# Splitting one product between VectorE and GpSimd, issuing two output matmuls earlier, and narrowing the last output piece

## The chip, the cores and the metric

The kernel runs on one core of a Trainium2 chip. The metric is the device time of one execution in microseconds; of several executions the median is given. The span in a profile is the time from the first to the last instruction of the profiled execution, about 1.8 us less than the device time of the same execution.

## The reference

An attention-like step feeds a two-layer block. Per batch (8) and head (8), with x of 512 x 64 and a state of 32 x 64:

```python
scores = scale * np.matmul(x, state.transpose(0, 1, 3, 2))
a = softmax(scores); xread = np.matmul(a, state)
scores2 = scale * np.matmul(state, x.transpose(0, 1, 3, 2))
a2 = softmax(scores2); sread = np.matmul(a2, x)
# rows of both, heads side by side: 4352 rows of 512
h = rows @ w_in                       # 512 -> 2048
g = h * (1.0 / (1.0 + np.exp(-h)))    # SILU
out = g @ w_out                       # 2048 -> 512
```

The softmax is shortened here; the rest is as in the reference, with the reshaping left out.

## The kernel before

The kernel folds the state into w_in ("W", one copy per batch), so that h is W times the normalised scores. G1 is the matmul of W with those scores, one step for each 128 of the 2048 hidden columns; G2 multiplies SILU(G1) by w_out and accumulates over the 16 steps. In batch 0 the whole chain has to start from nothing: load x, transpose, scores, exp, normalise, transpose, G1, SILU, G2. This ramp and the last output piece are what the change touches.

The normalisation; the argument `parts` says which engine multiplies which quarter:

```python
def norm(b, hg, parts=((nc.gpsimd, 0, 4),), nr=4):
    ...
    for c in range(0, 4, nr):
        nc.vector.tensor_reduce(rs[:, ds(c, nr)], e[:, ds(c, nr)], axis=AX, op=ADD)
    nc.vector.reciprocal(rc[:], rs[:])
    for eng, c, n in parts:
        eng.tensor_tensor(a[:, ds(c, n)], e[:, ds(c, n)],
                          rc[:, ds(c, n)].to_broadcast([128, n, 4, NS]), op=MULT)
```

The ramp of batch 0 (cut; `both` is VectorE for the first half and ScalarE for the second; `upto(k)` emits G1 steps until k of them have been emitted):

```python
norm(0, 0)                                  # first head half, on GpSimd
scores(0, 1, 2)
exps(0, 1)
norm(0, 1, ((nc.vector, 0, 4),), 2)         # second head half, on VectorE
...                                         # GpSimd issues weight and x loads
pss0 = w1_mms(0, [(128, 384)])
keep_busy(2, psH, "h1")                     # filler matmuls
for c in (0, 2):                            # transpose, copy out of PSUM
    ...; at_mms(ps_a, 0, 0, c, 2); copy(both[c // 2], aT[0][:, 0, ds(c, 2), :], ps_a[:])
for c in (0, 2):
    ...; at_mms(ps_a, 0, 1, c, 2); copy(nc.vector, aT[0][:, 1, ds(c, 2), :], ps_a[:])
w1_out(0, [(128, 128)], both, pss0)         # W for the second G1
upto(1)                                     # first G1: four steps of 256, two SILU halves
w1_out(0, [(128, 256)], (nc.vector, nc.vector), pss0, 128)
upto(2)                                     # second G1
for ft in range(12):
    upto(min(ft + LEAD0[ft], ready))
    ...
    for tt in range(3):
        G2(0, tt, ft)
```

The end:

```python
store(B, 0, nc.scalar)
last_cols(B, 1, 0, 256, nc.scalar, nc.sync)     # columns from, count, copy engine, queue
last_cols(B, 1, 256, 128, nc.vector, nc.scalar)
last_cols(B, 1, 384, 128, nc.vector, nc.sync)
```

The softmax here doesn't subtract the row's maximum and nothing guards it: scores larger than these inputs give would overflow.

## Time and profile before

| | before |
|---|---|
| device time, first three runs | 212.91 us (212.73 to 213.1) |
| span of the profile | 210.9 us |
| PE busy | 205.3 us (97%) |
| start of the third G1 (the end of the ramp) | 12.88 us |
| start of the last three pieces on PE | 203.95 us |
| issue of the last store | 208.00 us |

PE is busy nearly without a break, so the busy table alone says little. The profile's lines give start, duration, engine, source line, operation, output and inputs with their shapes, and a count. PE is TensorE's matmuls and PEld its weight loads, DVE is VectorE, ACT is ScalarE, POOL is GpSimd; SPq and ACTq are the queues that issue DMAs. Brackets say how long the engine stood idle just before and who released it.

### The profile page before, as it was taken

The numbers are of one execution on the slowest core, as the hardware profiler recorded it, in microseconds if no ns is written. First come the engines' busy times: TensorE is split into PE (matmuls) and PEld (weight loads), VectorE is DVE, ScalarE is ACT, GpSimd is POOL, SyncE is SP. The second block draws the span as 40 slices with busy tenths as digits, with TensorE's granted clock in tenths as the row PEclk, the third lists the DMA queues.
The fourth block names the chain that finished last, engine by engine and source line by source line (L and its number), as shares of the span: only waits on it lengthen the run. The fifth ranks groups of instructions, "written<-read, shape, count | busy, mean of one in ns | idle before, by whom it ended". The sixth has DMA issues, their size and how long they took to land.

```text
span 210.9 us, 3866 instructions
## 1 busy us (share of the span) xinstructions
PE 205.3 (97%) x1575; PEld 96.8 (46%) x1575; DVE 74.0 (35%) x146; ACT 139.2 (66%) x244; POOL 39.5 (19%) x62
## 2 busy tenths in 40 slices
PE   7899999999999999999999999999999999999993
PEld 2444354445444444444444544444444444466653
DVE  3851268567831336115211662043412306100011
ACT  3865677899577867697569855996775166644410
POOL 8681213704220402021201202000200000000000
PEclk9999999999999999999999999999999999999999
DMA  6999999995559475644925528115321111011112
GB/s 205 181 204 206 284 256 354 219 273 194 101 145 259 152 137 119 145 154 114 237 75 173 112 71 193 50 50 102 85 64 46 63 56 53 0 50 50 53 50 99
DMA packets 42929, 28.65 MB, mean 136 GB/s; under 512 B 28064, under 2 KB 37792, under 8 KB 42912
## 3 DMA queue, kind: packets, MB, share of 16 engines
q1 hardware_dynamic: 36720, 20.65, 37.7%
q0 software_dynamic: 5904, 7.64, 17.5%
q8 instruction: 12, 0.20, 0.4%
q10 hardware_dynamic: 288, 0.13, 0.2%
q14 instruction: 5, 0.04, 0.1%
HBM read 17.43 MB, written 8.91 MB: 125 GB/s over the span
## 4 chain that ended last, share of the span: by engine, by line
PE 95%; DMA 2%; DVE 1%; ACT 0%; issue 0%; DVEq 0%
PE o L566 51%; PE h L525 26%; PE ps_w L469 4%; PE h L546 3%; PE o_a L566 3%; DMA x_f<-in_x_dram 2%; PE o_part L588 2%; PE ps_sr L416 1%; PE ps_xt L253 1%; PE ps_sc L306 1%; PE ps_scT L332 1%; PE ps_busy L165 1%; PE ps_at L398 0%; PE h L507 0%; DVE W L159 0%; ACT xT L157 0%
## 5 line engine op out<-in xcount | busy, mean ns | idle before, releaser
L566 PE MATMUL o<-w_out_sb,g 128*128 128x512 bf16 x496 | 131.8, 379 | 0.0
L557 ACT ACTIVATE g<-h 128x512 bf16<-128x512 f32 (+1 forms) x143 | 81.2, 573 | 34.2 <-PE h L525 20.1
L566 PEld LDWEIGHTS <-g 128*128 128x128 bf16 x528 | 50.3, 98 | 59.0 <-issue 3.8
L525 PE MATMUL h<-aT,W 128*128 128x512 bf16 x254 | 74.5, 379 | 0.1
L159 DVE COPY o_sb<-o 128x512 f32<-128x512 f32 x15 | 10.4, 691 | 89.8 <-PE o L566 87.3
L525 PEld LDWEIGHTS <-W 128*128 128x128 bf16 x254 | 24.6, 98 | 30.5 <-issue 1.2
L159 DVE CAST W<-ps_w 128x512 bf16<-128x512 f32 (+2 forms) x36 | 22.2, 659 | 23.2 <-PE ps_w L469 23.2
L157 ACT ACTIVATE W<-ps_w 128x512 bf16<-128x512 f32 (+1 forms) x32 | 16.2, 562 | 11.1 <-PE ps_w L469 11.1
L159 POOL CAST x_nat<-x_f 128x512 bf16<-128x512 f32 x24 | 14.2, 631 | 35.9 <-DMA x_f<-in_x_dram 35.9
L157 ACT ACTIVATE o_sb<-o 128x512 f32<-128x512 f32 x16 | 9.5, 597 | 14.3 <-PE o L566 11.8
L362 POOL TENSOR_TENSOR an<-e,rcn 128x512 bf16<-128x512 bf16 x5 | 7.6, 1518 | 48.9 <-DVE rcn L360 39.3
L469 PE MATMUL ps_w<-w_in_sb,stT 64*32 64x512 bf16 (+2 forms) x264 | 10.1, 373 | 0.0
L566 PE MATMUL o_a<-w_out_sb,g 128*128 128x512 bf16 x32 | 10.0, 379 | 0.0
L546 PE MATMUL h<-xmT,w_in_sb 128*128 128x256 bf16 x64 | 9.6, 273 | 0.0
L546 PEld LDWEIGHTS <-w_in_sb 128*128 128x128 bf16 x64 | 6.3, 98 | 3.9
L165 PE MATMUL ps_busy<-busy 128*128 128x512 bf16 x16 | 5.8, 481 | 1.2 <-DVE warm L172 1.2
L359 DVE TENSOR_REDUCE rs<-e 128x32 f32<-128x1024 bf16 x5 | 6.1, 1211 | 2.1 <-DMA e<-eT 2.1
L346 ACT ACTIVATE eT<-ps_scT 128x512 bf16<-128x512 f32 x10 | 5.4, 594 | 1.6 <-PE ps_scT L332 1.6
L786 ACT ACT_TABLE_LOAD x5 | 6.4, 1283 | 0.1
L382 POOL TENSOR_TENSOR an<-exp_nat,rc 128x512 bf16<-128x512 bf16 x3 | 3.1, 1047 | 13.9 <-DMA x_f<-in_x_dram 8.7
L469 PEld LDWEIGHTS <-stT 64*32 64x32 bf16 x264 | 3.2, 90 | 5.2 <-issue 3.9
L768 ACT ACT_TABLE_LOAD x4 | 5.1, 1283 | 0.1
(76 smaller groups left out, 99.8 us busy)
## 6 DMA issues: line engine op xcount, KB each, us to landing
out_dram<-o_sb SPq DMA_DIRECT2D x33, 256.0 KB, 2.4
x_f<-in_x_dram SPq DMA_DIRECT2D x4, 1024.0 KB, 6.3
x_f<-in_x_dram POOLq DMA_DIRECT2D x2, 1024.0 KB, 12.6
w_in_sb<-in_moe_w_in_dram POOLq DMA_DIRECT2D x3, 512.0 KB, 10.2
x_f<-in_x_dram SPq DMA_DIRECT2D x2, 512.0 KB, 4.7
w_out_sb<-in_moe_w_out_dram POOLq DMA_DIRECT2D x4, 256.0 KB, 11.9
w_out_sb<-in_moe_w_out_dram POOLq DMA_DIRECT2D x2, 512.0 KB, 12.1
x_f<-in_x_dram POOLq DMA_DIRECT2D x2, 512.0 KB, 14.9
```

Source lines behind the costliest of these rows:

```text
L157: nc.scalar.activation(dst, src, func=COPY, bias=0.0)
L159: eng.tensor_copy(dst, src)
L165: nc.tensor.matmul(ps[:], busy[:, 0:128], busy[:], start=True, stop=True, skip_group_check=True)
L346: nc.scalar.activation(t[:, hg], scT_ps[hg][:], func=EXP, bias=0.0, scale=SCALE)
L359: nc.vector.tensor_reduce(rs[:], e2[b][:], axis=AX, op=ADD)
L362: eng.tensor_tensor(a[:, hg], e2[b][:, hg], rc[:, hg].to_broadcast([128, 4, 4, NS]), op=MULT)
L469: nc.tensor.matmul(pss[f, hg][ds(32 * s, 32), 0:n], stT[ds(r, 64), b, h // 2, s % 2, :], w_in_sb[ds(r, 64), h // 2, ds(f, n)], start=True, ...
L525: nc.tensor.matmul(h_ps[k][:], W1[b][:, hg, ds(128 * ft, 128)], aT[b][:, hg, :, :], start=(hg == 0), stop=(hg == 1), skip_group_check=True,)
L546: nc.tensor.matmul(ps[:, 0:256], w_in_sb[:, kt, ds(128 * ft, 128)], xmT[:, :, kt].rearrange("p t n b -> p t (n b)"), start=(kt == 0), stop ...
L557: nc.scalar.activation(g[:, 0:n], ps[:, 0:n], func=SILU, bias=0.0)
L566: nc.tensor.matmul(outs[tt][:], gt[b * NFT + ft][:, ds(128 * tt, 128)], w_out_sb[:, ft, :], start=(ft == 0), stop=(ft == NFT - 1), skip_gr ...
L786: nc.scalar.activation(warm[:], busy[:, 0:1], func=SILU, bias=0.0)
```

## The change

The intent: VectorE has a queue of work in the ramp, so GpSimd takes half of its second product; the first two G2 steps need only the first half of the first SILU, so they go ahead of the second G1; the last output piece is halved so that less is left to copy and store after the last matmul.

```diff
-    norm(0, 1, ((nc.vector, 0, 4),), 2)
+    norm(0, 1, ((nc.vector, 0, 2), (nc.gpsimd, 2, 2)), 2)
 ...
-    w1_out(0, [(128, 128)], both, pss0)
+    w1_out(0, [(128, 128)], (nc.vector, nc.vector), pss0)
     upto(1)
     w1_out(0, [(128, 256)], (nc.vector, nc.vector), pss0, 128)
+    G2(0, 0, 0)
+    G2(0, 1, 0)
     upto(2)
+    G2(0, 2, 0)
 ...
     for ft in range(12):
-        upto(min(ft + LEAD0[ft], ready))
+        if ft > 0:
+            upto(min(ft + LEAD0[ft], ready))
 ...
-        for tt in range(3):
+        for tt in range(3 if ft > 0 else 0):
             G2(0, tt, ft)
 ...
-    last_cols(B, 1, 256, 128, nc.vector, nc.scalar)
-    last_cols(B, 1, 384, 128, nc.vector, nc.sync)
+    last_cols(B, 1, 256, 192, nc.vector, nc.scalar)
+    last_cols(B, 1, 448, 64, nc.vector, nc.sync)
```

## The prediction

> **What bounds the kernel now.** I read the page first: busy shares, then the chain that ended last.
>
> ```profile
> PE 205.3 (97%) x1575; PEld 96.8 (46%) x1575; DVE 74.0 (35%) x146; ACT 139.2 (66%) x244; POOL 39.5 (19%) x62
> PE 95%; DMA 2%; DVE 1%; ACT 0%; issue 0%; DVEq 0%
> ```
>
> TensorE sets the time: 95% of the chain is PE. A change can therefore only move three things: how long PE waits in the ramp before its unbroken stream begins, the PE work itself, and what follows its last matmul. The change touches the first and the last. I took the ramp (10 to 15 us) and the end apart in narrow windows of the timeline. The ramp, engine by engine:
>
> ```profile
> 9.07 1.05 POOL L382 TENSOR_TENSOR an<-exp_nat,rc 128x512 bf16<-128x512 bf16 x1 [2.00 <-DVE rc L380]
> 9.97 0.70 DVE L382 TENSOR_TENSOR an<-exp_nat,rc 128x512 bf16<-128x512 bf16 x1
> 10.43 0.69 PE L398 MATMUL ps_at<-ident,an 128*128 128x128 bf16 x8
> 10.74 0.80 DVE L159 COPY aT<-ps_at 128x256 bf16<-128x256 bf16 x3
> 11.45 0.94 DVE L159 CAST W<-ps_w 128x128 bf16<-128x128 f32 x3
> 11.70 0.66 ACT L516 ACTIVATE g<-h 128x256 bf16<-128x256 f32 x2 [0.21 <-PE h L507]
> ```
>
> Columns are start, duration, engine, line, operation. GpSimd normalises the first head half until 10.12, VectorE the second until 10.67, PE transposes both, and VectorE copies the transposes out (ACT takes one copy and one W copy, not in these lines). The first half of SILU ends at 11.70+0.38 = 12.08. What PE does meanwhile:
>
> ```profile
> 11.09 0.79 PE L507 MATMUL h<-aT,W 128*128 128x256 bf16 x4
> 11.79 0.60 PE L525 MATMUL h<-aT,W 128*128 128x512 bf16 x2
> 12.23 0.59 PE L566 MATMUL o<-w_out_sb,g 128*128 128x512 bf16 x2
> 12.67 0.38 PE L566 MATMUL o_a<-w_out_sb,g 128*128 128x512 bf16 x1
> 12.88 1.03 PE L525 MATMUL h<-aT,W 128*128 128x512 bf16 x4
> ```
>
> The reader should see that the second G1 (11.79) lies exactly in the wait for that SILU. It ends its issue at 11.79+0.44 = 12.23, and the first G2 follows without a hole, though its input has been ready since 12.08. I take 12.88, the start of the third G1, as the mark of the ramp: from there PE hardly waits.
>
> **What the Trainium skill says.** (1) "GPSIMD Engine Reference", § 4.1 Engine selection, calls GpSimd about twice as slow as VectorE for elementwise work on two inputs, and its § 1 Specifications says that its SBUF interfaces are shared with VectorE, with contention where a VectorE instruction has two SBUF inputs. The trace agrees in direction: this product takes 1.05 us on GpSimd against 0.70 us on VectorE (1.5 times). Where both start together (59.17 us, VectorE first), VectorE keeps 0.69 and GpSimd takes 1.55; where GpSimd is already running (34.18), VectorE is stretched to 0.88. (2) "TensorE: Matmul & The Clock Gate", § Back-to-back issue gap, gives N/2.4 + 2.5 ns a step, but about 81 ns for pairs of weight load and matmul at N=128. In this trace the smaller figure holds: eight transposes of 128 columns take 0.45 us of the chain (56 ns each), two 512-column steps 0.43 (216 ns each), and eight 64-column steps, each with its own weight load, 30.78 to 31.01 = 29 ns each. (3) "DMA: Bandwidth & Descriptors", § Specifications, asks for at least 512 B for line rate; the new last piece has rows of 64 x 4 = 256 B. The last stores before have 512 B rows and land in 1.9 to 2.0 us, so no run yet shows what that costs.
>
> **Part 1: GpSimd takes half of the second product.** VectorE's half is 256 columns. Halving the streamed part (512 columns at 0.96 GHz-like pace is about 0.53 of the 0.70 us) gives 0.43, so it ends at 9.97+0.43 = 10.40 instead of 10.67. GpSimd starts its half at 10.1 after its own first product: half of 1.05 plus a little is 0.55 us, but VectorE holds the two-input read until 10.40. From the pair at 59.17 GpSimd does about 0.1 us of work in such an overlap, so it ends near 10.85 (10.65 with no contention).
> What it buys: PE reaches the transposes at 10.43 in any case, because before them stand a W product that waited for w_in until 9.70 (0.29 us of issue) and two fillers (0.43). The first transpose copy on VectorE needs the transposes' end, 10.70, so it stays at 10.74. The second copy started at 11.05, held by the product's end at 10.67; now it can follow the first at VectorE's 0.21 us spacing, 10.95. The third needs GpSimd's end plus 0.38 (the distance from product end to copy start above, 10.67 to 11.05), 11.23 against 11.26. So one copy comes 0.10 us earlier. The first h is complete at about 11.56 instead of 11.66 and its SILU runs 11.60 to 11.98. Gain on this step: 0.10 us.
> GpSimd's six weight and x issues start 0.55 to 0.8 us later. I expect that to be hidden: the weight loads issued at 5.1, 10.1 and 11.6 us land 9.8, 10.2 and 13.8 us after issue, which is a backlog growing in the queue, not an issue limit.
>
> **Part 2: both first W copies on VectorE.** ACT loses a copy of 0.27 us that ended at 11.49, before its SILU could start, so ACT gains nothing. VectorE's W copies for the second G1 now end at about 11.65 and 11.9. That G1 could start near its old time for one half and about 11.95 for the other.
>
> **Part 3: two G2 steps ahead of the second G1.** PE issues the last first-G1 step by about 11.70 and then waits for SILU: first G2 at 11.98+0.05 = about 12.04. Then two G2 (0.43) to 12.47, second G1 (0.43) to 12.90, third G2 (0.22) to 13.12. The third G1 starts at 13.12 instead of 12.88: **+0.24 us**. The same matmuls are done, but 0.43 us of them have been taken out of a hole that they filled, and only 0.19 us of that is won back (0.10 from part 1, about 0.09 from the hole's other edges). Everything behind the mark is PE stream. The w_in block for the next W product landed at 5.14+9.8 = 14.94 and PE used it at 14.99, so a gain in the ramp of over 0.05 us could not have passed this load anyway; a loss meets no slack and goes through to the end.
>
> **Part 4: 192 + 64 columns at the end instead of 128 + 128.**
>
> ```profile
> 206.79 0.29 DVE L159 COPY o_part<-o_part 128x128 f32<-128x128 f32 x1 [5.40 <-PE o_part L588]
> 207.11 0.64 ACTq L598 DMA_DIRECT2D out_dram<-o_part  x1
> 207.68 0.29 DVE L159 COPY o_part<-o_part 128x128 f32<-128x128 f32 x1 [0.60 <-PE o_part L588]
> 208.00 0.54 SPq L598 DMA_DIRECT2D out_dram<-o_part  x1
> ```
>
> PE before: 32 steps x 56 ns = 1.79 us. After: 16 x 82.5 (the skill's formula, an estimate) + 16 x 29 = 1.78 us, the same. The last matmul's latency falls from 219 to 193 ns (the 64-column rows show 193): 0.03. The last copy falls from 0.29 to an estimated 0.23 us (64 columns fewer at about 1 ns): 0.07. The last store carries 32 KB instead of 64; 128 KB landed in 2.1 and 64 KB in 1.9 to 2.0 us, so 0 to 0.1 less. Sum **-0.12 us**. The 192-column piece is copied by about 207.61 and issued at 207.64 on ACT's queue, landing near 209.7, just under the last piece's 209.8: close, but not the bound.
>
> **Sum.** +0.24 - 0.12 = +0.12 us: 212.91 becomes about 213.0.
>
> **The rivals.** A, *the change works as meant*: the split product is worth its full 0.27 us, the SILU comes as much earlier, and PE no longer stops for W copies. For it: VectorE is busy without a break from 10.74 to 12.4, so shortening its queue looks right. Against: PE's 10.43 and the load at 14.94 are not moved by it. It would make 212.6. B, *GpSimd is late*: contention as at 59.17 puts its half at 10.95 or later, the third copy and the second SILU half slip, and the delayed load issues make the W product at 20.85 wait (its w_in landed at 10.07+10.2 = 20.27, slack 0.58). For it: the measured 1.55 us. Against: the backlog. It would make 213.3 to 213.6. C, *narrow matmuls cost a full weight load*: if the last 16 steps took 56 ns instead of 29, PE ends 0.43 later and the sum is 213.5. Against it stand the 29 ns score steps. D, *256 B rows make the last store slow*: up to +0.2 in place of the gain, 213.2.
>
> **Range and chances.** The terms are tenths of a microsecond against run-to-run scatter of 0.37 us (212.73 to 213.1). A pulls down by 0.4, B and C up by about 0.5; with scatter I take 212.5 to 213.4. Two per cent is 4.3 us, which no rival comes near: same 0.98, faster 0.01, slower 0.01.
>
> **What would show it right or wrong.** Right: first G2 at about 12.04 with PE idle before it until SILU ends, third G1 near 13.12, the W product that stood at 14.99 near 15.23, last copy near 0.23 us, last 16 matmuls at 29 ns. Wrong: the third G1 at or before 12.88 (then A), a PE wait on w_in at 21 us (B), the last piece's matmuls spread over 0.9 us (C), a landing of the last store over 2.1 us (D).

## The result and the profile after

The changed kernel took 212.99 us (212.93 to 213.15, six runs) against 212.82 us (212.73 to 213.1, six runs) for the kernel before. The ratio is 1.0008, 95% interval 0.9995 to 1.0021: the same within 2%. Ratios here are the mean time of one kernel's runs over that of the other's of the same rounds, so they are not quite the ratio of the medians quoted. By time alone a loss is likely but not certain; where it would come from is read from the trace. First the page of the changed kernel, busy table and chain:

```profile
PE 205.9 (98%) x1575; PEld 96.9 (46%) x1575; DVE 74.2 (35%) x147; ACT 139.1 (66%) x243; POOL 40.4 (19%) x63
...
PE 95%; DVE 1%; POOL 1%; issue 0%; ACT 0%; POOLq 0%
```

PE still is 95% of the chain. In the chain's account, POOL (GpSimd) has come in where a DMA stood before. The ramp in the timeline, VectorE, GpSimd and ACT:

```profile
9.97 0.42 DVE L382 TENSOR_TENSOR an<-exp_nat,rc 128x256 bf16<-128x256 bf16 x1
10.08 0.79 POOL L382 TENSOR_TENSOR an<-exp_nat,rc 128x256 bf16<-128x256 bf16 x1
...
10.68 0.86 DVE L159 COPY aT<-ps_at 128x256 bf16<-128x256 bf16 x3 [0.28 <-PE ps_at L398]
11.46 1.14 DVE L159 CAST W<-ps_w 128x128 bf16<-128x128 f32 x4
11.56 0.73 ACT L516 ACTIVATE g<-h 128x256 bf16<-128x256 f32 x2 [0.23 <-PE h L507]
```

VectorE's product now ends at 10.39, but GpSimd's half ends at 10.87, later than VectorE's whole product did before (10.67). VectorE then waits 0.28 us for PE's transposes, and its three copies end where they did. The first SILU starts 0.14 us earlier. What PE makes of it:

```profile
11.05 0.81 PE L507 MATMUL h<-aT,W 128*128 128x256 bf16 x4
...
11.99 0.10 PEld L566 LDWEIGHTS <-g 128*128 128x128 bf16 x1 [0.52 <-ACT g L516]
11.99 0.60 PE L566 MATMUL o<-w_out_sb,g 128*128 128x512 bf16 x2
12.44 0.59 PE L525 MATMUL h<-aT,W 128*128 128x512 bf16 x2
12.87 0.38 PE L566 MATMUL o_a<-w_out_sb,g 128*128 128x512 bf16 x1
13.08 1.03 PE L525 MATMUL h<-aT,W 128*128 128x512 bf16 x4
```

The last step of the first G1 starts at 11.60 and PE can give way about 0.11 us later, the distance of two such steps; then nothing is left that may run until SILU has ended at 11.94. The first G2 starts at 11.99 after a hole of some 0.28 us, and the third G1 at 13.08 instead of 12.88. That 0.20 us is still there at the start of the last three pieces: 204.16 instead of 203.95. The end of the changed kernel:

```profile
207.42 0.36 DVE L159 COPY o_part<-o_part 128x192 f32<-128x192 f32 x1 [5.83 <-PE o_part L588]
207.81 0.64 ACTq L598 DMA_DIRECT2D out_dram<-o_part  x1
207.89 0.23 DVE L159 COPY o_part<-o_part 128x64 f32<-128x64 f32 x1
208.14 0.54 SPq L598 DMA_DIRECT2D out_dram<-o_part  x1
```

Counted from the start of the last three pieces, the last issue comes 3.99 us later; before it was 208.00 - 203.95 = 4.05. So 0.07 us is gained up to the issue (3.988 against 4.054 unrounded). But the span ends 7.00 us after that start, before 6.97: the gain is gone. (The page gives spans to 0.1 us; these two come from the packed traces, 211.156 - 204.156 and 210.921 - 203.949.) The DMA issues of the end (size, and time from issue to landing), first before, then changed:

```profile
out_dram<-o_part ACTq DMA_DIRECT2D x1, 64.0 KB, 2.0
out_dram<-o_part SPq DMA_DIRECT2D x1, 64.0 KB, 1.9
```

```profile
out_dram<-o_part ACTq DMA_DIRECT2D x1, 96.0 KB, 2.1
out_dram<-o_part SPq DMA_DIRECT2D x1, 32.0 KB, 2.0
```

The last store carries half as much and takes longer to land, 2.0 us after its issue instead of 1.9 (1.99 and 1.89 in the packed traces). The DMA activity between 207.5 and 211.5 us, one digit for 0.1 us, shows a candidate for why; before and changed:

```profile
DMA  5998200006950000069500000000000000000000
```

```profile
DMA  0059983000000000699982000000000000000000
```

Before, the last two stores are two separate bursts. In the changed kernel they have become one.

### The profile page after: what moved, and what is told of

It is laid out like the page before. It is cut to its first block, busy times and chain, and to the rows that moved or that the text cites. A ratio compares the mean times of both kernels' runs of the same rounds, so it can differ in the third digit from the quotient of the medians.

```text
span 211.2 us, 3868 instructions
## 1 busy us (share of the span) xinstructions
PE 205.9 (98%) x1575; PEld 96.9 (46%) x1575; DVE 74.2 (35%) x147; ACT 139.1 (66%) x243; POOL 40.4 (19%) x63
## 4 chain that ended last, share of the span: by engine, by line
PE 95%; DVE 1%; POOL 1%; issue 0%; ACT 0%; POOLq 0%
PE o L566 51%; PE h L525 26%; PE ps_w L469 4%; PE h L546 3%; PE o_a L566 3%; PE ps_busy L165 2%; PE o_part L588 2%; PE ps_sr L416 1%; POOL an L382 1%; PE ps_scT L332 1%; PE ps_sc L306 1%; PE ps_xt L253 1%; DVE xT L159 0%; PE ps_at L398 0%; DVE W L159 0%
## 5 line engine op out<-in xcount | busy, mean ns | idle before, releaser
L165 PE MATMUL ps_busy<-busy 128*128 128x512 bf16 x16 | 6.4, 520 | 1.2 <-DVE warm L172 1.2
L382 POOL TENSOR_TENSOR an<-exp_nat,rc 128x512 bf16<-128x512 bf16 (+1 forms) x4 | 3.9, 983 | 15.2 <-ACT eT L346 9.7
```

Source lines behind the costliest of these rows:

```text
L165: nc.tensor.matmul(ps[:], busy[:, 0:128], busy[:], start=True, stop=True, skip_group_check=True)
L382: eng.tensor_tensor(a[:, ds(c, n)], e[:, ds(c, n)], rc[:, ds(c, n)].to_broadcast([128, n, 4, NS]), op=MULT,)
```

## The experiments

**My theory:** the change of order costs 0.3 us because the second G1 had filled the wait for SILU; the split gives back only a part; and the end gives nothing because the last store queues behind the one ahead of it. **Rivals:** GpSimd's late half causes the loss of the ramp; the W copies on VectorE do; the last store is slow because of its 256-byte rows.

One thing had to be settled first. The profiles do not begin their ramp at the same moment: x arrives at different times in different executions, and the start of VectorE's second product ranges from 9.97 to 10.89 us over the profiles here. So I compare the ramp from that start. These are the marks of the kernels that differ in the ramp, with e4 as a control:

| kernel | VectorE's second product starts | first G2 | third G1 | third G1 minus product start |
|---|---|---|---|---|
| before | 9.97 | 12.23 | 12.88 | 2.91 |
| changed | 9.97 | 11.99 | 13.08 | 3.11 |
| e1, order only | 10.62 | 12.78 | 13.87 | 3.25 |
| e2, order undone | 10.37 | 12.64 | 13.29 | 2.92 |
| e3, split only | 10.62 | 12.88 | 13.53 | 2.91 |
| e4, end only (ramp as before) | 10.34 | 12.60 | 13.25 | 2.91 |
| e6, early W copy | 10.08 | 12.13 | 12.78 | 2.70 |
| e7, e6 and swapped W products | 10.28 | 12.33 | 12.98 | 2.70 |

e4 has the ramp of before and an x that came 0.37 us later, and its difference is the same to 0.01 us; so is that of e8 (2.91, product at 10.89). The measure holds as long as the W product ahead of the transposes starts well before VectorE's product, 0.28 to 0.33 us in the rows above and longer in e8. In e9 and e10, whose ramp is that of before too, it started later than VectorE's product, because its w_in block arrived late, and the difference is 3.14 and 3.34; so they are left out here.

### e1: the order alone

```diff
     w1_out(0, [(128, 256)], (nc.vector, nc.vector), pss0, 128)
+    G2(0, 0, 0)
+    G2(0, 1, 0)
     upto(2)
+    G2(0, 2, 0)
```

(and the two edits of the loop, as in the change)

> Only the new order (two G2 steps ahead of the second G1), everything else as before. My theory (the order empties a hole that the second G1 filled): first G2 near 12.13, third G1 near 13.2 instead of 12.88 (+0.3 us), all of it kept to the end, about +0.3 us in time. Rival (the loss of the whole change comes from GpSimd's late half): third G1 stays at 12.88 or earlier and the time is that of before.

Timeline of e1, the product and PE's ramp:

```profile
10.62 0.69 DVE L382 TENSOR_TENSOR an<-exp_nat,rc 128x512 bf16<-128x512 bf16 x1
...
12.78 0.60 PE L566 MATMUL o<-w_out_sb,g 128*128 128x512 bf16 x2 [0.26 <-ACT g L516]
13.22 0.59 PE L525 MATMUL h<-aT,W 128*128 128x512 bf16 x2
13.66 0.38 PE L566 MATMUL o_a<-w_out_sb,g 128*128 128x512 bf16 x1
13.87 1.03 PE L525 MATMUL h<-aT,W 128*128 128x512 bf16 x4
```

PE waits for SILU ("ACT g"), and the ramp is 3.25 - 2.91 = 0.34 us longer. The time was 213.72 us against 213.27 (ratio 1.0034, interval 1.0006 to 1.0062), slower clear of noise, though two of its six runs stood a microsecond above the others (214.74 and 214.77), so the trace's 0.34 is the better size.

### e2: the changed kernel with the old order

```diff
-    G2(0, 0, 0)
-    G2(0, 1, 0)
     upto(2)
-    G2(0, 2, 0)
```

(and the two edits of the loop undone)

> The changed kernel with the old order of G1 and G2; split product, W copies on VectorE and the 192+64 end stay. My theory: first G2 near 12.2 and third G1 at 12.80 to 12.90, as before; time equal to before within 0.1 us. Rival (GpSimd's late half costs the time): third G1 stays near 13.08 and the time stays about +0.15 us.

```profile
10.37 0.42 DVE L382 TENSOR_TENSOR an<-exp_nat,rc 128x256 bf16<-128x256 bf16 x1
...
11.96 0.38 ACT L516 ACTIVATE g<-h 128x256 bf16<-128x256 f32 x1 [0.24 <-PE h L507]
...
12.19 0.29 PEld L525 LDWEIGHTS <-W 128*128 128x128 bf16 x2 [0.32 <-DVE W L159]
12.20 0.60 PE L525 MATMUL h<-aT,W 128*128 128x512 bf16 x2
12.64 0.59 PE L566 MATMUL o<-w_out_sb,g 128*128 128x512 bf16 x2
```

With the order undone the ramp is back at 2.92, although GpSimd's half and both W copies on VectorE are still there. Both of those rivals fall. SILU starts 1.59 us after the product, as in the changed kernel and 0.14 earlier than before, but the second G1 starts at 12.20 - 10.37 = 1.83, as before (1.82): it waits for its W copy on VectorE, and G2 stands behind it. The time was 213.18 against 213.27 us, ratio 1.0009 (0.9980 to 1.0037), which by itself tells nothing at this size.

### e3: the split alone

```diff
-    norm(0, 1, ((nc.vector, 0, 4),), 2)
+    norm(0, 1, ((nc.vector, 0, 2), (nc.gpsimd, 2, 2)), 2)
```

> Only the split of the second product between VectorE and GpSimd. My theory: the first SILU half starts near 11.56 instead of 11.70, but the second G1 still waits for its W copy and the third G1 stays at 12.80 to 12.88: time equal to before within 0.1 us. Rival A (the split is worth its full 0.27 us): third G1 near 12.6 and 0.2 us less. Rival B (GpSimd late hurts): third G1 past 12.95.

The ramp takes 2.91 us, as before; the second G1 starts at 12.44 - 10.62 = 1.82, as before. Ratio 1.0002 (0.9981 to 1.0023). So the split is worth nothing to the ramp in the old order and, by e1 against the changed kernel, 3.25 - 3.11 = 0.14 us in the new one. (The changed kernel also has both W copies on VectorE; but in e3, with the split alone, SILU already starts 0.14 us earlier after the product than before, 1.59 against 1.73, and in the new order it is SILU that the first G2 waits for.) The parts do not add up; each is worth what the wait that ends last lets through.

One thing in e3's profile has another cause. Its last pieces start 204.77 - 10.62 = 194.15 us after VectorE's product, in the kernel before 203.95 - 9.97 = 193.98, though the ramp is as long. The hole is at 18.97, where G2 is the first to use a block of w_out: it started 0.59 us after the G1 step ahead of it instead of 0.43, and the block had landed at 18.93. So what reaches the end of one profile can swing by 0.17 us with the arrival of a load; e6 below meets the same block.

### e5: GpSimd does both halves

```diff
-    norm(0, 1, ((nc.vector, 0, 4),), 2)
+    norm(0, 1, ((nc.gpsimd, 0, 2), (nc.gpsimd, 2, 2)), 2)
```

> GpSimd does both halves of the second product and VectorE none, so no half meets a VectorE product. If the 0.79 us of GpSimd's half in the changed kernel is contention with VectorE's half, each half here takes 0.52 to 0.58 us. Rival (a half simply costs that much on GpSimd, a large fixed part): each takes near 0.79 us.

Instructions that touch this tile in e5, with minimum, median and maximum duration in ns:

```profile
L382 POOL TENSOR_TENSOR an<-exp_nat,rc x3: 612/613/1050, 9.1 to 10.7; 128x256 bf16<-128x256 bf16 x2, 128x512 bf16<-128x512 bf16 x1
```

The half takes 0.61 us when VectorE does no product, 0.79 us beside VectorE's half. So 0.18 us is contention with that product. VectorE's other work in the ramp does not do it: GpSimd's second half in e5 ran beside VectorE's copies of the transposes (10.69 to 11.37) and took the same 0.61. VectorE's own half takes 0.42 to 0.43 us in every profile of a split kernel, but always beside GpSimd, so whether it is slowed too is not shown. The half alone is more than I expected: by 1.05 us for 512 columns and 0.61 for 256, an estimate gives 0.18 us fixed and 1.7 ns a column. Third G1 at 13.29, with a reciprocal that started at 9.69 as in the changed kernel: 0.4 us worse than before.

### e6 and e7: what the split needs to pay

In e6 VectorE uses the pause that the split opens (10.39 to 10.68 in the changed kernel) to copy the first half of W, and half of the second G1 goes between the steps of the first:

```diff
+    copy(nc.vector, W1[0][:, 0, ds(128, 128)], pss0[128, 0][:, 0:128])
     for c in (0, 2):                        # transposes of the scores
 ...
-    w1_out(0, [(128, 128)], both, pss0)
+    copy(nc.scalar, W1[0][:, 1, ds(128, 128)], pss0[128, 1][:, 0:128])
     upto(1)
 ...
     def g1_first():
 ...         # after the step i == 1, hg == 0
+                if i == 1 and hg == 0:
+                    g1_half(1, 0)
 ...         # in emit_G1
-            g1_half(k, 0)
+            if k > 1:
+                g1_half(k, 0)
             g1_half(k, 1)
```

(with the split of e3; `upto(2)` then issues the other half; G2 in the old order)

> Split product; VectorE copies the first W half in its pause before the transposes' copies (ACT the other, as before); half of the second G1 goes between the steps of the first G1, its other half right behind them; G2 after, as in the old order. My theory (the order is right when the filler for the SILU wait is ready early): third G1 2.65 to 2.75 us after the start of VectorE's second product, against 2.91 before and 3.11 changed; but the next W product must wait for its w_in block, so of the 0.2 us at most 0.1 to 0.15 reaches the end. Rival (VectorE's queue or GpSimd's half sets the ramp whatever the order): 2.9 again, no gain.

```profile
11.59 0.38 PE L527 MATMUL h<-aT,W 128*128 128x512 bf16 x1
11.81 0.27 PE L507 MATMUL h<-aT,W 128*128 128x256 bf16 x1
11.91 0.38 PE L527 MATMUL h<-aT,W 128*128 128x512 bf16 x1
12.13 0.59 PE L569 MATMUL o<-w_out_sb,g 128*128 128x512 bf16 x2
12.56 0.38 PE L569 MATMUL o_a<-w_out_sb,g 128*128 128x512 bf16 x1
12.78 1.03 PE L527 MATMUL h<-aT,W 128*128 128x512 bf16 x4
```

The second G1 (11.59 and 11.91) now fills two waits, and the ramp takes 2.70 us, 0.21 less than before. The early copy and the interleaving were not run apart, so how much each gives is open. Yet the time was 212.77 against 212.77 us (ratio 1.0000, 0.9986 to 1.0013). The last pieces start at 203.97; before with e6's x, 0.11 us later, they would have started at 204.06, so 0.09 of 0.21 is left. Most of the rest can be seen in the timeline of e6:

```profile
17.64 0.59 PE L527 MATMUL h<-aT,W 128*128 128x512 bf16 x2
18.18 0.59 PE L569 MATMUL o<-w_out_sb,g 128*128 128x512 bf16 x2
```

Two such steps take 0.43 us, so G2 could have started at 18.07; it started at 18.18. The block of w_out that this step is the first to use was issued at 5.87 and landed 12.3 us later, at 18.14. The profile names no releaser for this hole; I read it from the two times, and e3's hole at the same step fits. The w_in block that I had named as the gate landed at 14.87, and the W product started at 14.91, a few hundredths late at most.

e7 also swaps the order of two W products, so that the one whose block is long there goes first:

```diff
+            if ft == 2:
+                pss1 = w1_mms(1, [(W1_AT[ft], 512)], new_h)
             pss = w1_mms(0, [W0[ft]])
-            if ft in W1_AT:
+            if ft == 6:
                 pss1 = w1_mms(1, [(W1_AT[ft], 512)], new_h)
```

> As e6, and the W product of batch 1, whose w_in block is already there, goes ahead of the one of batch 0. If the w_in block gated e6, the start of the 16 steps of W products comes without a hole and 0.2 us reaches the end: time about 0.2 us under before. If it did not, e7 equals e6. A loss would mean that the batch-1 product waits for its state copies on VectorE.

The ramp is 2.70 again; the last pieces start at 204.07, where x's 0.31 us of delay would have put them at 204.26 in the kernel before: 0.19 us is kept, in one profile and with e3's swing of 0.17 us in mind. Time 212.73 against 212.77 us, ratio 0.9996 (0.9984 to 1.0009), no proof by itself. In this profile w_out landed at 5.87 + 11.7 = 17.6, in time, so e7 does not show that the swap is what kept the gain; that stays open.

### e4, e8, e9, e10: the end

e4 is the kernel before with the changed end only:

> Only the last pieces of 192 and 64 columns. As I predicted it: last copy 0.225 us, last issue 0.07 to 0.1 us earlier counted from the start of the last pieces, span and time 0.1 us less. Rival, which the changed kernel's trace suggests: the last store lands 2.0 us after its issue instead of 1.9, which gives the gain back, and the time is that of before.

e8 has pieces of 384, 64 and 64 columns, e9 of 320, 128 and 64:

```diff
-    last_cols(B, 1, 0, 256, nc.scalar, nc.sync)
-    last_cols(B, 1, 256, 128, nc.vector, nc.scalar)
-    last_cols(B, 1, 384, 128, nc.vector, nc.sync)
+    last_cols(B, 1, 0, 320, nc.scalar, nc.sync)      # e8: 0, 384
+    last_cols(B, 1, 320, 128, nc.vector, nc.scalar)  # e8: 384, 64
+    last_cols(B, 1, 448, 64, nc.vector, nc.sync)     # e8: the same
```

> The kernel before with last pieces of 384, 64 and 64 columns: the store in front of the last one carries 32 KB instead of 96 KB. If the last store of the changed kernel lands 0.1 us later because it queues behind the 96 KB, it lands in 1.9 us or less here. If it is the 256-byte rows, it stays at 2.0 us.

> The kernel before with last pieces of 320, 128 and 64 columns: the store ahead of the last one carries 64 KB in 512-byte rows and should be through before the last one's bytes start. If the 2.0 us landing of the 64-column store is queueing behind the store ahead of it, it lands in 1.9 us here; if it is its 256-byte rows or a floor, it stays at 2.0 us.

e10 has e4's pieces and leaves out the store of the middle one (`if f != 256:` ahead of the store), with a wrong output:

> The kernel before with the 192 and 64 column pieces, and the 192-column piece copied but not stored, so its part of the output is wrong on purpose. The last store then has the DMA engines to itself. Queueing theory: it lands in 1.8 to 1.9 us. Row-length theory: it stays at 2.0 us, and the span from the start of the last pieces stays at 7.0 us.

| kernel | store ahead of the last one | start of the last pieces to last issue | last store, issue to landing | start of the last pieces to span end |
|---|---|---|---|---|
| before (last store 64 KB) | 64 KB, 0.89 us earlier | 4.05 | 1.89 | 6.97 |
| changed | 96 KB, 0.33 us earlier | 3.99 | 1.99 | 7.00 |
| e4 | 96 KB, as in the changed kernel | 3.99 | 1.98 | 7.00 |
| e8 | 32 KB, 0.46 us earlier, and 192 KB, 0.67 us earlier | 3.99 | 2.00 | 7.03 |
| e9 | 64 KB, 0.39 us earlier | 3.99 | 1.82 | 6.85 |
| e10 | none stored | 3.99 | 1.83 | 6.92 |

The last two columns are from the packed traces, which hold times to the nanosecond. Over all profiles of this case the last column is 6.97 to 7.00 with the end of before (six profiles) and 6.99 to 7.03 with the changed end (four). The landing is 1.98 to 1.99 in those four, and 1.81 to 1.83 in e9, e10 and e11.

The last store, from the DMA issues; the line is the same in e9 and in e10:

```profile
out_dram<-o_part SPq DMA_DIRECT2D x1, 32.0 KB, 1.8
```

Alone, or behind 64 KB issued 0.39 us earlier, the same 32 KB in the same 256-byte rows land in 1.8 us; behind 96 KB issued 0.33 us earlier they take 2.0. e10 against e4 differs in nothing but that store, so the row-length rival falls: the store ahead costs the last one 0.16 us. That it does so by queueing fits the single burst seen above. e8 was badly chosen: its 384-column piece leaves so late that 192 KB stand ahead of the last store, so it tells only that the queue can form there too. e4's time was 213.15 against 213.27 us (ratio 0.9994, 0.9973 to 1.0015): the end alone changes nothing that can be measured in time. e10's span ends 0.08 us earlier than e4's, half of what its last store lands earlier; the other half stays unexplained.

### e11 and e12: a version that beats both

e11 is e7's ramp with e9's end, and e12 the changed kernel once more in the same rounds.

> The ramp of e7 (split product, early W copy, interleaved second G1, swapped W products) with the end of e9 (320, 128 and 64 columns). From the traces the ramp is worth 0.19 us and the end about 0.05: 0.25 us under before, a ratio near 0.9988, which the interval may just miss; the third G1 2.70 us after VectorE's second product starts. If the ramp gain is lost to the arrival of the weight blocks, the ratio is 1.000.

> The changed kernel once more, in the same rounds as e11: ratio near 1.001 to 1.0015 (0.2 us from the ramp, nothing from the end), the third G1 3.11 us after the start of VectorE's second product, the last store landing 2.0 us after its issue.

e11 took 212.72 us and e12 213.33 us against 213.05 for the kernel before: ratios 0.9982 (0.9969 to 0.9996) and 1.0014 (0.9998 to 1.0029). e11 is faster than the kernel before clear of noise, by 0.3 us between the medians. The changed kernel's interval holds 1 again, as in its first comparison. In both profiles the w_in block ahead of the transposes was late (that W product started at 10.43 and 10.33), so the mark of the table fails there, and my expected 2.70 and 3.11 did not show. From the start of that W product to the third G1 they take 3.02 and 3.44 us, as e6 and e7 (3.03 each) and the changed kernel (3.44) did. The fair comparison is with e9 and e10, which have the ramp of before and had the block late too: 3.10 us each. So in these profiles e11's ramp gains 0.08 us instead of 0.21, and the changed one loses 0.34, all that the order cost in e1: the first SILU starts 1.92 us after the late W product in all four, so the split gives nothing back when that block is the last to come. How often it is late in the timed runs is not known. The last stores of e11 and e12 landed after 1.8 and 2.0 us, and their spans end 6.85 and 6.99 us after the start of the last pieces, as in e9 and the changed kernel.

## Why the prediction was right

The time (213.0 predicted, 212.99 measured) and the verdict were right, the first partly by luck: +0.12 us was predicted, on top of the 212.91 us of the first three runs; all six gave 212.82 us, so +0.17 was measured between the medians, and +0.24 between the two profiled spans. By its own steps:

- **Part 3, the order.** Right in mechanism and nearly in size. First G2 12.04 predicted, 11.99 measured; third G1 13.12, measured 13.08; the W product 15.23, measured 15.18: +0.20 us where I had +0.24. e1 shows that the order alone costs 0.34.
- **Part 1, the split.** The end of GpSimd's half was predicted near 10.85 and was 10.87, from terms each slightly off: the half alone takes 0.61 us, not 0.55, and contention adds 0.18 where the prediction has 0.20. VectorE's half took 0.42 as predicted (0.69 us for 512 columns and 0.42 for 256 put the streamed part of 512 near 0.53 us). What the split gives back was 0.14 us instead of 0.10, because the first copy started at 10.68, not 10.74, and pulled the second along. Those 0.06 us are not the split's doing: the w_in block for the W product ahead of the transposes landed at 9.53 instead of 9.65, and in e1 and e4, without the split, the first copy came as early after VectorE's product (0.71 us). That its late load issues would be hidden held: the w_in block issued at 10.82 instead of 10.07 landed at 20.2 instead of 20.3.
- **Part 2, the W copies.** Right: e2 has them, e3 has not, and both ramps are as long as before. e3's SILU starts as early as the changed kernel's, so ACT gained nothing from losing its copy.
- **The load at 14.94.** I wrote that a gain in the ramp of over 0.05 us could not pass it. That is too strong: it holds for the arrival times of that one profile. In e6 x came 0.11 us later and this block 0.08 us earlier, and the W product started 4.83 us after VectorE's product instead of 5.02, so 0.19 had passed; what held e6 up then was, by the times, the w_out block at 18.14.
- **Part 4, the end.** This step failed. Of its -0.12 us the shorter copy (0.07) came true. The shorter latency of the last matmul did not show: the last copy starts 3.73 us after the last pieces begin in both kernels. "0 to 0.1 less" for the last store was 0.1 more: I had seen that the two stores come close, but asked only which lands last, not whether one delays the other. Rival D's effect came, with another cause than the rows that it named: e10 has the same rows and lands in 1.8 us. In all the end came out at +0.03 us (6.97 to 7.00).

So the sum of +0.12 was a ramp 0.04 too dear and an end 0.15 too cheap; both errors are smaller than the scatter of single runs. Rival A (the change works as meant) fell with the third G1 past 12.88; B with the W product that it names, which started at 21.05 instead of 20.85, no more delayed than the third G1; and C with the PE end: the last 64-column steps did not stretch it (3.70 us for the last pieces in both).

## What to carry to other kernels

Before moving an instruction ahead of another on an in-order engine, ask what the other was filling: here two matmuls that were "ready first" emptied a wait, and the ramp became shorter than before only when the filler's own input was made ready early. Measure a ramp from an event inside it, not from the start of the trace, when the first loads arrive at varying times. When the last piece is made smaller, look at the store ahead of it: here 96 KB issued 0.33 us ahead took back what the smaller piece gained, and 64 KB issued 0.39 us ahead did not.

## What the Trainium skill lacked or had wrong

- "GPSIMD Engine Reference", § 1 Specifications and § 4.1 Engine selection: the contention with two-input VectorE instructions has no size in these sections (the page "SBUF — State Buffer" treats it too; the runs here were not compared with it). Here a 256-column product takes 0.61 us alone and 0.79 us beside a VectorE product that overlaps its first 0.31 us. The page's "~2× slower for 2-input ops" was 1.05 against 0.70 us, 1.5 times, at 512 columns.
- "TensorE: Matmul & The Clock Gate", § Back-to-back issue gap: about 81 ns for a weight load and matmul pair at N=128; the pairs here take 56 ns, and 29 ns at 64 columns.
- "DMA: Bandwidth & Descriptors", § Queues, rings and completion order: it tells how the engines take turns between queues, but not what it costs a small store. Here 32 KB issued 0.33 us behind 96 KB from another queue land in 2.0 us, alone in 1.8. For the 512 B that the prediction cites, no penalty was visible at this size: 32 KB in 256-byte rows landed in 1.8 us, 64 KB in 512-byte rows in 1.9; no run has 32 KB in 512-byte rows to compare.
- No page that I read says how much the arrival of a kernel's first loads varies: the instruction that depends on x started between 9.97 and 10.89 us over these profiles, and the w_out block issued at 5.87 to 5.96 landed between 17.2 and 18.9, which is more than everything this change moves.
